# Retention and two MoE layers in one kernel: one tile per PSUM bank, w_out's combinations in layer 1, and more elementwise work on GpSimd

## The chip, the cores and the metric

One core of a Trainium2 chip runs the whole program. The metric is the device time of one execution in microseconds. The engines are named as in the profile: PE is TensorE, DVE is VectorE, ACT is ScalarE, POOL is GpSimd, SP is the engine whose queue issues almost all DMAs here.

## The reference

Three stages in a row, all in float32 (batch 4, 8 heads, 768 positions, head size 64, so 3072 tokens of 512 features; the hidden size of both layers is 2048):

```python
state = gamma * state + k_t (outer) v_t          # retention, per head, position by position
y_t   = scale * q_t @ state
h = y @ w_in;  P = a0 + a1*h + a2*h*h + a3*h**3;  Q = 1 + |b0|*|h| + |b1|*h*h     # layer 1
x = (P / (Q + 1e-6)) @ w_out
h = x @ w_in2;  g = h * clip(h + 3, 0, 6) / 6                                     # layer 2
out = g @ w_out2
```

The layer weights arrive as float64 and are rebuilt on the chip from their two 32-bit words.

## The kernel before, in words

**Split operands.** A factor is kept as a rounded high part (`hi`, made by ACT with a copy) and a rest (`lo` = value minus `hi`, made by one `tensor_tensor` subtract). A product is three matmuls: hi by hi, hi by lo, lo by hi.

**Layer 1.** Tokens are taken in six blocks of 512, the hidden size in 16 pieces of 128. A *step* is one piece of one block; there are 96 steps, written out by the main loop (line 1133 on), which in step n issues: 12 matmuls for h of step n (`emit_h`), ACT's three reads of the h before (`s1_h`), DVE's three operations for the gate of step n-2 (`s1_g`, lines 449 to 451), ACT's hi of that g (`s_hi`, line 456), then `s1_pq` (lines 434, 435, 438) with `s_lo` between its parts, which is the subtract that gives g's rest `gl` (line 462, on DVE), and 12 matmuls of step n-2 into the four output banks (`emit_o`, line 391). The last four of these 12 read `gl`; in the last step of a block they are interleaved, so that the third one reads it. The retention's chunks (`att_...`) and the rebuilding of layer 1's weights (`w_...`) are laid between the steps through the tables `begin`, `middle`, `between`, `before` and `after`: a call put there for step n is issued at that place of step n. Engines run what is issued to them strictly in order.

**Preparation of layer 2's weights.** Layer 2 uses a seven-product scheme on 2 by 2 halves of tokens, input and hidden pieces, so combinations of quarters of `w_in2` and `w_out2` are needed, each as hi and lo, and are stored to DRAM (`win_d`, `wout_d`). A half unit is: two loads (`prep_load`), one ACT operation (`prep_scale`), two on DVE (`prep_bits`, lines 559 and 560), four 128x128 sums on POOL (`prep_sums`), the hi copies on ACT (`prep_hi`) and the subtracts (`prep_lo`, line 601). For `w_in2` (16 half units) this is done in layer 1, five half units in the 16 steps from 32, 48 and 64 on and one at step 83, with the subtracts on DVE (two of 128x512). For `w_out2` (16 half units, in batches of 2 to 3) it is done in the first pair of layer 2, with the subtracts on POOL (one of 128x1024).

**Layer 2.** Blocks go in three pairs. `xc_load`, `xc_sums` and `xc_split` make the token combinations of a pair (for the first pair during steps 81 to 92, for the others late in the pair before). Then eight *units* (`unit`, hidden piece u of 8) make the gates: 7 groups of 6 matmuls (`mm1`, line 655) into PSUM banks A, B, C, D, with DVE sums of banks in between (line 531 through `tensor`) and a gate per quarter (`relu` on ACT, line 673; `gate` on DVE, line 679). A and D are the two halves of one tile, `live[p]` (profile name `ad`). Then come 14 *halves* of products, in the order `ORDER` = 1, 5, 6, 7, 3, 2, 4 with k = 0, 1; each is 48 matmuls of 128x256 (line 797). `g_split` makes the operand of a half two halves ahead: for each of four pieces j a source, then hi on ACT (line 771), then lo on DVE (line 531). For q = 5, 6, 7 and 3 the source is itself a sum or difference, made on DVE by `source` (line 758) just before. `evac` combines the banks into the output, and its place on DVE is between the splits:

```python
for i, (q, k) in enumerate(halves):
    product(p, q, k)
    if i: evac(p, *halves[i - 1])
    if i + 2 < len(halves): g_split(p, *halves[i + 2])
```

**PSUM** has eight banks: `accA` and `accB` (one tile of two banks each), `h` (two tiles of one), `at` (one tile of two). In layer 2 the product accumulators A and B lie in `accA` and `accB`, and C in `at`.

Of the kernel before, what the change touches and what calls it, by code (L numbers as in the profile page):

```python
# [16 lines left out]
CH = 128  # L17
# [15 lines left out]
def tile_retention_moe_moe2(  # L33
# [292 lines left out]

    def att_xh(blk, c):
        y = attn[blk, c][0].rearrange("p (e j t) -> p e j t", e=2, t=CH)[:, :, 0:2, :]
        xs = slice(c * CH, (c + 1) * CH)
        if blk == VIA:  # L330
            xf = o_p.tile([128, 512], F32, tag="osb", name=f"xf{blk}_{c}")
            nc.scalar.activation(split(by_pair(xf)), y, AF.Copy)
            nc.sync.dma_start(out=x_dram[:, :, xs].rearrange("a p t -> p a t"), in_=by_pair(xf))
        else:
            if c == 0:
                x_tiles(blk)
            nc.scalar.activation(split(xin[blk][0][:, :, xs]), y, AF.Copy)  # L337
# [35 lines left out]
    def emit_o(key):  # L373
# [241 lines left out]
    def xc_sums(p, c, which):  # L615
# [79 lines left out]
    def unit(p, u, part):  # L695
        nm = f"{p}_{u}"
        if part == 0:
            if u == 0:
                live[p] = ps_at.tile([128, 1024], F32, tag="at", name=f"ad{p}")
            now = live[p, u] = {"A": live[p][:, 0:512], "D": live[p][:, 512:1024]}  # L700
# [8 lines left out]
            tensor(nc.vector, now["U2"], now["B"], now["s1"], ALU.add)  # L709
            if u:  # L710
# [4 lines left out]
        else:  # L715
# [8 lines left out]
            gate(p, 22, u, h22, relu(h22, "22_" + nm))  # L724
            mm1(p, u, 4, now["D"], True)
# [18 lines left out]
    def source(p, q, k, j):  # L744
# [77 lines left out]
    def evac(p, q, k):  # L822
        ps = accs[p, BANK[q]][:, k * 512 : (k + 1) * 512]
# [7 lines left out]
        elif q == 7:  # L831
# [3 lines left out]
            scaled(o, accs[p, "C"][:, k * 512 : (k + 1) * 512], kept["U3", k])  # L835
# [37 lines left out]
    def wo_bits(v):  # L873
        for u, s in wo_batches[v] if v < len(wo_batches) else ():
# [3 lines left out]

    def wo_split(v):
        for u, s in wo_batches[v] if v < len(wo_batches) else ():  # L880
            hi = take(f"hwo{u}_{s}")
            prep_hi("wo", u, s, 2, hi)
            prep_lo("wo", u, s, nc.gpsimd)
            give(hi, *wo_rooms.pop((u, s)))

    def second_layer():
        for p in range(PAIRS):
            for u in range(NU):
                last = u == NU - 1
                if (p, u) != (0, 0):  # L890
                    unit(p, u, 0)
                    if not last:
                        win_load(p, u + 1)
                    if p == 0:
                        wo_load(u + 1)
                        wo_bits(u)
                    unit(p, u, 1)
                    if p == 0:
                        wo_split(u)
                if last:  # L900
                    wout_load(p, ORDER[0])
                    g_split(p, 1, 0, range(3))
            mm1(p, NU - 1, 3, live[p, NU - 1]["C"], False)
            last_two(p, NU - 1, 0)
            last_two(p, NU - 1, 1)
            g_split(p, 1, 0, (3,))
            give(*(t for q in ORDER for t in xs.pop((p, q))))
            jobs_x = xc_jobs(p + 1) if p + 1 < PAIRS else []
            g_split(p, *halves[1])
            for i, (q, k) in enumerate(halves):  # L910
# [8 lines left out]
                for fn, *args in jobs_x.pop(0) if i >= 7 and jobs_x else ():  # L919
# [5 lines left out]
    def xc_jobs(p):  # L925
        js = []
# [344 lines left out]
```

## Time and profile before

| what | us |
|---|---|
| median of 3 runs (lowest to highest) | 1313.13 (1311.78 to 1315.44) |
| the profiled execution's own time | 1309.85 |
| its span, first to last instruction | 1308.1 |
| PE busy | 1151.9 (88%) |
| DVE busy | 973.9 (74%) |
| ACT busy | 731.3 (56%) |
| POOL busy | 139.6 (11%) |
| mean granted clock of TensorE | 0.958 |

The profile is that of one execution; times in its rows count from the span's start. Layer 1's steps end near 657 us, the three pairs of layer 2 end near 901, 1105 and 1303 us. A row of a timeline gives start, duration, engine, line, operation, what it writes and reads, and in brackets the idle time of the engine before it and what ended that. A busy PE is not PE at its peak. The granted clock is the share of full speed.

### The profile page before, as it was taken

Reading aid. Unit: us, or ns where it says so; the run is one execution under the profiler, and the core shown is the slowest. Engines: PE = TensorE matmul, PEld = TensorE weight load, DVE = VectorE, ACT = ScalarE, POOL = GpSimd, SP = SyncE. Lnnn points to the kernel's source line nnn. Section 1 sums busy time; section 2 is a strip of 40 time slices with the busy share of each in tenths; the row PEclk is TensorE's granted clock in tenths of the full one; section 3 lists DMA queues with packets and bytes.
Section 4 is the critical chain, followed back from the end, with each engine's and each line's share of the span. In section 5 each row is a group of like instructions: output and inputs, shape, how many; then the busy total and the mean of one; then the engine's idle time right before and its main releaser. Section 6 shows DMA issues by size and latency. Waiting matters only on the chain.

```text
span 1308.1 us, 18580 instructions
## 1 busy us (share of the span) xinstructions
PE 1151.9 (88%) x6748; PEld 958.6 (73%) x6748; DVE 973.9 (74%) x1514; ACT 731.3 (56%) x1309; POOL 139.6 (11%) x179
## 2 busy tenths in 40 slices
PE   8789999999999999998985679778888779888878
PEld 5567888887788777786764568677677779667778
DVE  6898999989989889999874456675556675556663
ACT  3999888677777777777653334342224343233341
POOL 0221110011101101200037550000000000000000
PEclk9899999999999999999997789989999989999989
DMA  9898444134344434434439996348733437832433
GB/s 340 244 249 219 103 114 145 47 132 131 128 136 154 129 106 147 136 105 145 129 104 339 335 316 211 127 135 303 285 113 106 152 113 234 330 128 98 162 112 113
DMA packets 133099, 224.13 MB, mean 171 GB/s; under 512 B 9744, under 2 KB 75408, under 8 KB 133008
## 3 DMA queue, kind: packets, MB, share of 16 engines
q1 hardware_dynamic: 128832, 215.35, 49.2%
q0 software_dynamic: 4176, 7.60, 3.5%
q8 instruction: 53, 0.87, 0.3%
q14 instruction: 38, 0.31, 0.1%
HBM read 167.08 MB, written 48.23 MB: 165 GB/s over the span
## 4 chain that ended last, share of the span: by engine, by line
PE 38%; DVE 31%; ACT 16%; issue 7%; DMA 6%; SPq 1%; POOL 0%; ACTq 0%; DVEq 0%; POOLq 0%
PE h L370 8%; PE ad L655 5%; PE hB L655 5%; ACT s L771 5%; DVE s L531 4%; PE accA L391 4%; PE hC L655 4%; PE accB L391 4%; DVE S L531 3%; PE mA L797 3%; DVE p L450 2%; DVE u L435 2%; DVE u L449 2%; PE mC L797 2%; DVE p L434 2%
## 5 line engine op out<-in xcount | busy, mean ns | idle before, releaser
L370 PE MATMUL h<-xh,wi 128*128 128x512 f32 x768 | 211.4, 397 | 0.9 <-ACT xh L337 0.9
L370 PEld LDWEIGHTS h<-xh,wi 128*128 128x128 f32 x768 | 141.5, 188 | 34.2 <-issue 2.8
L797 PE MATMUL mB<-wo,s 128*128 128x256 f32 x864 | 118.8, 298 | 25.5 <-issue 15.5
L391 PE MATMUL accA<-gh,wo 128*128 128x512 f32 x384 | 122.4, 400 | 16.7 <-ACT gh L456 16.0
L797 PEld LDWEIGHTS mB<-wo,s 128*128 128x128 f32 x864 | 113.0, 204 | 30.8 <-issue 20.4
L391 PE MATMUL accB<-gh,wo 128*128 128x512 f32 x384 | 119.4, 392 | 0.0
L655 PE MATMUL ad<-x,wih 128*128 128x512 f32 x160 | 52.4, 448 | 59.2 <-DVE U L531 39.5
L771 ACT ACTIVATE s<-S 128x512 fp32r<-128x512 f32 x72 | 45.5, 631 | 103.9 <-DVE S L531 103.9
L370 PE MATMUL h<-xl,wi 128*128 128x512 f32 x384 | 103.3, 391 | 0.0
L797 PE MATMUL mC<-wo,s 128*128 128x256 f32 x576 | 82.7, 310 | 21.5 <-DVE o L820 10.6
L391 PEld LDWEIGHTS accA<-gh,wo 128*128 128x128 f32 x384 | 70.5, 189 | 40.8 <-ACT gh L456 27.4
L797 PEld LDWEIGHTS mC<-wo,s 128*128 128x128 f32 x576 | 80.5, 219 | 23.4 <-ACT s L771 12.2
L443 ACT ACTIVATE r<-u,cst 128x512 f32<-128x512 f32 x96 | 69.3, 722 | 46.9 <-DVE u L435 46.9
L531 DVE TENSOR_TENSOR s<-S,s 128x512 fp32r<-128x512 f32 x72 | 49.9, 693 | 52.1 <-ACT s L771 52.1
L456 ACT ACTIVATE gh<-p 128x512 fp32r<-128x512 f32 x96 | 60.6, 632 | 47.2 <-DVE p L451 47.2
L655 PEld LDWEIGHTS ad<-x,wih 128*128 128x128 f32 x160 | 31.3, 208 | 75.2 <-DVE U L531 47.6
L673 ACT ACTIVATE r<-U,cst 128x512 f32<-128x512 f32 x48 | 34.6, 721 | 92.1 <-DVE U L531 92.1
L391 PEld LDWEIGHTS accB<-gh,wo 128*128 128x128 f32 x384 | 72.7, 189 | 15.7
L370 PEld LDWEIGHTS h<-xl,wi 128*128 128x128 f32 x384 | 72.4, 189 | 15.9
L434 DVE TENSOR_TENSOR p<-p,h 128x512 f32<-128x512 f32 x96 | 65.6, 683 | 23.6 <-ACT u L428 23.4
L797 PE MATMUL mA<-wo,s 128*128 128x256 f32 x576 | 75.5, 292 | 6.7 <-ACT s L771 3.1
L797 PEld LDWEIGHTS mA<-wo,s 128*128 128x128 f32 x576 | 73.1, 199 | 9.1 <-ACT s L771 4.2
(163 smaller groups left out, 2438.8 us busy)
## 6 DMA issues: line engine op xcount, KB each, us to landing
wo<-wout SPq DMA_DIRECT2D x84, 512.0 KB, 6.0
wih<-win SPq DMA_DIRECT2D x48, 512.0 KB, 6.8
wil<-win SPq DMA_DIRECT2D x48, 512.0 KB, 7.1
T<-in_qk_t_dram SPq DMA_DIRECT2D x48, 256.0 KB, 4.6
rwi<-in_moe_w_in_dram SPq DMA_DIRECT2D x16, 512.0 KB, 5.2
rwo<-in_moe_w_out_dram SPq DMA_DIRECT2D x16, 512.0 KB, 5.1
kv<-in_kv_dram SPq DMA_DIRECT2D x32, 256.0 KB, 5.4
pwi<-in_moe_w_in_dram SPq DMA_DIRECT2D x32, 256.0 KB, 4.3
```

The lines of the kernel that those rows point to most:

```text
L370: nc.tensor.matmul(ps, lhsT=w[:, cs], rhs=x[:, c, :], start=n == 0, stop=n == 3 * KD - 1)
L391: nc.tensor.matmul(acc[layer, blk][j], lhsT=l, rhs=r, start=f == f0 and i == 0, stop=f == f1 and i == 2)
L434: nc.vector.tensor_tensor(out=p, in0=p, in1=h, op=ALU.mult)
L435: nc.vector.scalar_tensor_tensor(out=u, in0=s, scalar=babs[:, 1:2], in1=u, op0=ALU.mult, op1=ALU.add)
L443: nc.scalar.activation(r, u, AF.Ln, scale=1.0 / LN_SCALE, bias=ln_bias)
L449: nc.vector.scalar_tensor_tensor(out=u, in0=u, scalar=Q_CONST, in1=r, op0=ALU.add, op1=ALU.mult)
L456: nc.scalar.activation(gh, tm[key], AF.Copy)
L531: engine.tensor_tensor(out=out, in0=a, in1=b, op=op)
L655: nc.tensor.matmul(bank, lhsT=wl[p, u][c][a][:, slot], rhs=xs[p, q][b][:, c * 512 : (c + 1) * 512], start=start and i == 0 and c == 0, sto ...
L673: nc.scalar.activation(r, h, AF.Relu, bias=three)
L771: nc.scalar.activation(hi, src, AF.Copy)
L797: nc.tensor.matmul(out, lhsT=l, rhs=r, start=q in (1, 4, 5, 6) and t == 0 and f == 0 and i == 0, stop=f == NU - 1 and i == 2, skip_group_c ...
```

## The change

Six edits:

1. **Banks.** The four output banks of layer 1 become four tiles `acc0` to `acc3`; in layer 2 the accumulators A and B lie in these by half k, and C in the two `h` tiles. D of a unit gets the tile `acc0`, apart from A, except in the very first unit. Retention's first block uses `acc0` to `acc3` too, so that its copies and masks over two banks become two instructions each.
2. **g's rest** (`s_lo`) goes from DVE to POOL, in all 96 steps.
3. **Preparation.** `prep_lo` of `w_in2` goes from DVE to POOL and writes new tiles of the pool `osb` (3 buffers) and not in place. The half units go faster (nine per 16 steps), and 15 of the 16 half units of `w_out2` follow in layer 1: 10 among the same steps up to 78 and five at steps 82 to 90. One is left for the first pair.
4. **Token combinations** (`xc_sums`) go from DVE to POOL; their loads come earlier, and their splits are spread three to a half.
5. **Half of g's sums** (`source`, j = 1 and 3) go from DVE to POOL.
6. **Order.** A unit is issued in three parts where it was two, cut after U2; the last piece of the first split comes before the last unit's closing operations.

The core of the diff:

```diff
     def two_banks(blk, i, name):
...
+        if blk == 0 and i < 2:
+            banks = [ps_acc.tile([128, 512], F32, tag=f"acc{2 * i + e}", name=f"{name}_{e}") for e in range(2)]
+            return banks, banks
...
     def emit_o(key):
...
-                t[:, i * 512 : (i + 1) * 512]
-                for t in (ps_acc.tile([128, 1024], F32, tag=f"acc{s}", name=f"acc{s}{layer}_{blk}_{f}") for s in "AB")
-                for i in range(2)
+                ps_acc.tile([128, 512], F32, tag=f"acc{j}", name=f"acc{layer}_{blk}_{f}_{j}") for j in range(KD)
...
     def s_lo(key):
-        nc.vector.tensor_tensor(out=gl, in0=tm.pop(key), in1=gh.bitcast(F32), op=ALU.subtract)
+        nc.gpsimd.tensor_tensor(out=gl, in0=tm.pop(key), in1=gh.bitcast(F32), op=ALU.subtract)
...
-    def prep_lo(kind, u, s, engine):
+    def prep_lo(kind, u, s, engine, in_place=False):
...
+        for part, (at, hi) in enumerate(done):
+            cs = slice(at, at + 512)
+            if in_place:
+                lo = raw[:, cs]
+            else:
+                lo = o_p.tile([128, 512], F32, tag="osb", name=f"lo{kind}{u}_{s}_{part}")
+            tensor(engine, lo, raw[:, cs], f32(hi), ALU.subtract)
+            prep_store(kind, u, s, cs, 1, lo)
...
     def unit(p, u, part):
...
-                live[p] = ps_at.tile([128, 1024], F32, tag="at", name=f"ad{p}")
-            now = live[p, u] = {"A": live[p][:, 0:512], "D": live[p][:, 512:1024]}
+                live[p] = ps_at.tile([128, 1024], F32, tag="at", name=f"a{p}")
+            now = live[p, u] = {"A": live[p][:, 0:512]}
...
+            if (p, u) == (0, 0):
+                now["D"] = live[p][:, 512:1024]
+            else:
+                now["D"] = ps_acc.tile([128, 512], F32, tag="acc0", name="hD" + nm)
             mm1(p, u, 4, now["D"], True)
...
     def source(p, q, k, j):
-            tensor(nc.vector, to, a, b, op)
+            tensor(nc.gpsimd if j % 2 else nc.vector, to, a, b, op)
...
     def product(p, q, k):
-        if k == 0 and q in (1, 6, 5):
-            pool, tag = {"A": (ps_acc, "accA"), "B": (ps_acc, "accB"), "C": (ps_at, "at")}[b]
-            accs[p, b] = pool.tile([128, 1024], F32, tag=tag, name=f"m{b}{p}")
+        if q in (1, 6, 5):
+            pool, tag = {"A": (ps_acc, f"acc{k}"), "B": (ps_acc, f"acc{2 + k}"), "C": (ps_h, "h")}[b]
+            accs[p, b, k] = pool.tile([128, 512], F32, tag=tag, name=f"m{b}{p}_{k}")
...
     def second_layer():
...
                     unit(p, u, 0)
+                    unit(p, u, 1)
                     if not last:
                         win_load(p, u + 1)
                     if p == 0:
-                        wo_load(u + 1)
-                        wo_bits(u)
-                    unit(p, u, 1)
+                        wo_load(u)
+                        wo_bits(u - 1)
+                    unit(p, u, 2)
                     if p == 0:
-                        wo_split(u)
+                        wo_split(u - 1)
...
+        js = {5: [(xc_load, p, 0)], 6: [(xc_load, p, 1)]}
...
+            js[7 + c] = [(xc_sums, p, c, 0, nc.gpsimd), (xc_sums, p, c, 1, nc.gpsimd)]
...
-    starts = [b + i for b in (32, 48, 64) for i in (3, 5, 8, 10, 12)] + [83]
...
+    halves_due = [(kind, u, i) for kind in ("wi", "wo") for u in range(NU) for i in range(2)]
+    starts = [b + i for b in (32, 48, 64) for i in (2, 3, 5, 6, 8, 9, 11, 12, 14)][1:]
+    for n, job in zip(starts, halves_due):
+        put(begin, n, prep_load, *job)
+        put(middle, n + 1, prep_scale, *job)
+        put(between, n + 1, prep_bits, *job)
+        put(before, n + 1, prep_sums, *job)
+        put(before, n + 1, prep_hi, *job, 0)
+        put(middle, n + 2, prep_hi, *job, 1)
+        put(before, n + 2, prep_lo, *job, nc.gpsimd)
+    wo_units = halves_due[len(starts) :]
+    wo_batches = {n: [wo_units.pop(0)[1:]] for n in (-14, -12, -10, -8, -6, 1)}
+    for n in (-14, -12, -10, -8, -6):
...
+    for c, n in enumerate((84, 89)):
+        put(begin, n, xc_load, 0, c)
+        put(before, n + 1, xc_sums, 0, c, 0, nc.gpsimd)
+        put(before, n + 2, xc_sums, 0, c, 1, nc.gpsimd)
```

## Rows read from the trace of the kernel before

**Rows 1.** Busy time by stretch: length; PE, PEld, DVE, ACT, POOL; granted clock; DMA share.

```profile
core 0: us, PE busy (x) PEld busy (x) DVE busy (x) ACT busy (x) POOL busy (x), PEclk, DMA share, GB/s
...
244.10:559.00 314.90, 306.63 (x1858) 245.19 (x1857) 286.55 (x443) 232.87 (x441) 37.06 (x60) 1.00 0.39 129
569.90:657.20 87.30, 79.86 (x337) 62.05 (x337) 79.16 (x124) 61.97 (x105) 2.45 (x4) 1.00 0.37 121
...
674.40:791.00 116.60, 83.33 (x301) 64.38 (x301) 62.06 (x92) 48.48 (x71) 69.71 (x72) 0.82 1.03 319
791.00:901.00 110.00, 91.65 (x673) 88.35 (x673) 76.24 (x121) 42.20 (x74) 0.00 (x0) 0.92 0.49 169
901.00:994.00 93.00, 80.19 (x336) 63.50 (x336) 46.69 (x71) 26.59 (x41) 0.00 (x0) 0.98 0.54 198
994.00:1105.40 111.40, 92.92 (x674) 89.90 (x672) 76.72 (x122) 42.67 (x75) 0.00 (x0) 0.91 0.46 159
...
1196.10:1303.20 107.10, 90.48 (x673) 87.33 (x671) 63.23 (x100) 35.07 (x61) 0.00 (x0) 0.92 0.40 133
```

**Rows 2.** Timeline of PE in layer 1: the first matmuls of two neighbouring steps.

```profile
216.87 1.07 PE L370 MATMUL h<-xh,wi 128*128 128x512 f32 x4
...
222.31 1.07 PE L370 MATMUL h<-xh,wi 128*128 128x512 f32 x4
```

**Rows 3.** Waits of the whole span: us in total, times, longest.

```profile
ACT s L771 <- DVE S L531: 103.9, 71, 2.9
...
PE ad L655 <- DVE U L531: 39.5, 19, 5.7
```

**Rows 4.** Timeline of PE, second pair: first and last unit that waits.

```profile
914.68 1.20 PE L655 MATMUL ad<-x,wih 128*128 128x512 f32 x4 [1.51 <-DVE U L531]
...
982.98 1.19 PE L655 MATMUL ad<-x,wih 128*128 128x512 f32 x4 [1.57 <-DVE U L531]
```

**Rows 5.** Timeline of PE, first pair: the start of two of its units.

```profile
710.46 0.77 PE L655 MATMUL ad<-x,wih 128*128 128x512 f32 x1 [6.92 <-DMA wih<-win]
...
778.07 2.07 PE L655 MATMUL ad<-x,wih 128*128 128x512 f32 x4 [3.53 <-DVE U L531]
```

**Rows 6.** Timeline of DVE, second pair, split of a half with q = 7.

```profile
1036.77 0.69 DVE L531 TENSOR_TENSOR s<-g,s 128x512 fp32r<-128x512 f32 x1 [0.78 <-ACT s L771]
1037.38 0.69 DVE L531 TENSOR_TENSOR g<-g,g 128x512 f32<-128x512 f32 x1
1038.77 0.69 DVE L531 TENSOR_TENSOR s<-g,s 128x512 fp32r<-128x512 f32 x1 [0.70 <-ACT s L771]
```

**Rows 7.** Timeline of PE, second pair: halves (7, 0), (7, 1), (3, 0), (3, 1).

```profile
1044.22 7.46 PE L797 MATMUL mB<-wo,s 128*128 128x256 f32 x48 [5.16 <-issue]
1052.99 5.99 PE L797 MATMUL mB<-wo,s 128*128 128x256 f32 x48 [1.31 <-DVE e L820]
1062.23 8.53 PE L797 MATMUL mC<-wo,s 128*128 128x256 f32 x48 [3.25 <-issue]
1074.89 7.47 PE L797 MATMUL mC<-wo,s 128*128 128x256 f32 x48 [4.12 <-DVE o L820]
```

**Rows 8.** Groups by line: busy us, mean ns of one, idle before.

```profile
L462 DVE TENSOR_TENSOR gl<-p,gh 128x512 fp32r<-128x512 f32 x96 | 65.8, 685 | 11.9 <-ACT gh L456 11.8
L434 DVE TENSOR_TENSOR p<-p,h 128x512 f32<-128x512 f32 x96 | 65.6, 683 | 23.6 <-ACT u L428 23.4
```

**Rows 9.** The same view: POOL's subtracts and sums.

```profile
L531 POOL TENSOR_TENSOR pwo<-pwo,hwo 128x1024 f32<-128x1024 f32 x16 | 39.8, 2513 | 0.0
L531 POOL TENSOR_TENSOR pwi<-pwi 128x128 f32<-128x128 f32 x64 | 39.5, 638 | 362.4 <-DVE pwi L560 329.7 <-ACT r L443 31.4
```

**Rows 10.** Timelines of POOL and DVE, near 293 and 781 us.

```profile
292.46 3.07 POOL L531 TENSOR_TENSOR pwi<-pwi 128x128 f32<-128x128 f32 x4 [12.77 <-DVE pwi L560]
292.85 0.74 DVE L438 SCALAR_TENSOR_TENSOR p<-p,ab,h 128x512 f32<-128x512 f32 x1
294.27 0.95 DVE L449 SCALAR_TENSOR_TENSOR u<-u,r 128x512 f32<-128x512 f32 x1
...
777.69 4.72 POOL L531 TENSOR_TENSOR pwo<-pwo,hwo 128x1024 f32<-128x1024 f32 x2
781.08 1.89 DVE L679 SCALAR_TENSOR_TENSOR g<-r,U 128x512 f32<-128x512 f32 x1 [3.06 <-DMA wout<-hwo]
```

More of the change, by code (lines that the diff above doesn't have):

```diff
@@ L325, in split, with outputs @@
         return t.rearrange("p (e j) t -> p e j t", e=2)
+    def outputs(blk, c, to):
+        banks = attn[blk, c][0]
+        if len(banks) == 1:
+            y = banks[0].rearrange("p (e j t) -> p e j t", e=2, t=CH)
+            return [(y[:, :, 0:2, :], split(to))]
+        return [(by_pair(b)[:, 0:2, :], to[:, 2 * e : 2 * e + 2, :]) for e, b in enumerate(banks)]
     def att_xh(blk, c):
-        y = attn[blk, c][0].rearrange("p (e j t) -> p e j t", e=2, t=CH)[:, :, 0:2, :]
         xs = slice(c * CH, (c + 1) * CH)
@@ L336, in att_xh @@
                 x_tiles(blk)
-            nc.scalar.activation(split(xin[blk][0][:, :, xs]), y, AF.Copy)
+            to = xin[blk][0][:, :, xs]
+        for y, x in outputs(blk, c, to):
+            nc.scalar.activation(x, y, AF.Copy)
+        if blk == VIA:
+            nc.sync.dma_start(out=x_dram[:, :, xs].rearrange("a p t -> p a t"), in_=by_pair(xf))
     def att_xl(blk, c):
-        both = attn[blk, c][0]
         if blk != VIA:
-            y = both.rearrange("p (e j t) -> p e j t", e=2, t=CH)[:, :, 0:2, :]
-            xh, xl = (split(x[:, :, c * CH : (c + 1) * CH]) for x in xin[blk])
-            nc.vector.tensor_tensor(out=xl, in0=y, in1=xh.bitcast(F32), op=ALU.subtract)
+            xh, xl = (x[:, :, c * CH : (c + 1) * CH] for x in xin[blk])
+            for (y, h), (_, lo) in zip(outputs(blk, c, xh), outputs(blk, c, xl)):
+                nc.vector.tensor_tensor(out=lo, in0=y, in1=h.bitcast(F32), op=ALU.subtract)
     def att_state(blk, c):
@@ L613, in xc_load, with xc_sums @@
         xraw[p, c] = [a, b]
-    def xc_sums(p, c, which):
+    def xc_sums(p, c, which, engine):
         a, b = xraw[p, c][:2]
@@ L709, in unit @@
             tensor(nc.vector, now["U2"], now["B"], now["s1"], ALU.add)
+        elif part == 1:
+            now = live[p, u]
             if u:
@@ L873, in wo_bits @@
     def wo_bits(v):
-        for u, s in wo_batches[v] if v < len(wo_batches) else ():
+        for u, s in wo_batches.get(v, ()):
             prep_scale("wo", u, s)
@@ L877, in wo_bits, with wo_done @@
             prep_sums("wo", u, s)
+    def wo_done(v):
+        give(*wo_rooms.pop(wo_batches[v][0]))
     def wo_split(v):
-        for u, s in wo_batches[v] if v < len(wo_batches) else ():
+        for u, s in wo_batches.get(v, ()):
             hi = take(f"hwo{u}_{s}")
             prep_hi("wo", u, s, 2, hi)
-            prep_lo("wo", u, s, nc.gpsimd)
+            prep_lo("wo", u, s, nc.gpsimd, True)
             give(hi, *wo_rooms.pop((u, s)))
@@ L918, in second_layer @@
                     g_split(p, *halves[i + 2])
-                for fn, *args in jobs_x.pop(0) if i >= 7 and jobs_x else ():
+                for fn, *args in jobs_x.get(i, ()):
                     fn(*args)
@@ L1043, in tile_retention_moe_moe2 @@
     put(before, 94, win_load, 0, 1)
-    put(before, 95, wo_load, 0)
-    put(before, N1, wo_load, 1)
-    put(before, N1 + 1, wo_bits, 0)
-    put(after, N1 + 1, wo_split, 0)
     nc.scalar.preload_act_table_set("natural_log_exp_and_others")
@@ L1187, in tile_retention_moe_moe2 @@
         if not cur:
-            unit(0, 0, n - N1)
+            unit(0, 0, 2 * (n - N1))
         o = at_step(n - LAG)
@@ L1193, in tile_retention_moe_moe2 @@
                 late.append(o)
+        if n == N1:
+            unit(0, 0, 1)
         for fn, *args in after.get(n, ()):
```

70 lines of the change are left out of this document (29 added, 41 removed).

## Prediction, made before the changed kernel was run

> **What bounds the kernel now.** I read the busy time by stretch first. In layer 1 (the stretches 244 to 559 and 570 to 657 of [rows 1]) PE is busy 306.6 of 314.9 us and 79.9 of 87.3: layer 1 is nearly PE's, with 8.3 and 7.4 us to gain. A step without retention takes 5.44 us for 24 matmuls [rows 2], 0.227 us each. DVE is at 91% there, so it is close behind. Layer 2 is another matter. A pair's eight units hold 336 matmuls (76.2 us at 0.227) and its 14 halves 83.9 us at the 5.99 us of an undisturbed half (the one at 1052.99 in [rows 7]); the rows show 93.0 and 111.4 us for the second pair, and 116.6 us for seven units of the first with a granted clock of 0.82 [rows 1].
>
> Then the waits tell what stands in PE's way. In the units PE waits for DVE's U, 39.5 us in all [rows 3]. The unit's first matmuls go to bank A, yet the wait ends when DVE has read bank D of the unit before: a wait between two halves of one tile. It comes once in each of seven units of the second pair, from the first to the last of [rows 4], 1.5 to 1.6 us each, and the same in the third pair. In the first pair waits are longer and partly for a weight load [rows 5]: there the DMAs run at full share, 1.03 [rows 1], because w_out2 is loaded and stored beside them.
>
> In the products DVE sets the pace. In a half with q = 5, 6, 7 or 3 each piece goes source (DVE), hi (ACT), lo (DVE), in order, and DVE idles 0.70 to 0.78 us while ACT makes hi [rows 6]; one piece takes 2.0 us (1036.77 to 1038.77), a half 8.0 us against PE's 5.99. ACT waits as long for the sources, 103.9 us in all [rows 3]. PE's stalls of 5.16 and 3.25 us follow, and after a stall a half takes 7.46 to 8.53 us, not 5.99 [rows 7].
>
> **The change part by part**, against the profiled execution's 1309.85 us.
>
> *D apart from A.* The wait for D's reader goes. Next to come on A would be the reader of bank A's last gate, three groups of matmuls (18 x 0.227 = 4.1 us) earlier by the code's order, and DVE's and ACT's work in a unit (nine and five operations of about 0.7 us) fits in 9.5 us. So a unit goes to 42 x 0.227 = 9.5 us from 11.38 (982.98 less 914.68, over 6). I count the seven idle times of 1.57 alone: **-11 in the second and in the third pair, -22**. Bounds: -18 (part comes back as a wait for hi copies) to -26 (7 x 1.86 x 2).
>
> *First pair's units.* All but one half unit of w_out2 leaves. Seven units at 9.5 are 67 us; the loads for the third unit are issued behind layer 1's last stores, which I price at 6 us, just under the worst load wait of 6.92 [rows 5]. So 73 where 116.6 stood: **-44**. Bounds -47 (no such wait) and -36 (two of them). With the DMAs gone the U waits of 3.5 us stay covered by D's tile; in the very first unit D still shares A's tile and that wait stays.
>
> *Half of g's sums on POOL.* Now two pieces of four keep 2.0 us and two cost DVE only their lo, 0.61 us apart [rows 6]: a half is 5.2 us, eight halves 42 where 64 stood, -22 for a pair. POOL's sources are not free. No row shows POOL on 128x512. Half of a 128x1024 piece is 1.26 us, four 128x128 ones are 2.55 [rows 9]; I take 1.26, since 1024 elements cost four times, not eight times, as much as 128, so long pieces are the cheaper. Two per half lie beside DVE's idle 0.7 us and delay the next lo by about 0.5 us each (next paragraph): +8 for eight halves. Late halves cost less after that: halves (3, 0) and (3, 1) took 4.0 us over 5.99 each and waited 4.1 more [rows 7]; I give that 4 us. **-18 a pair, -54** in all. Bounds: the products can't go below 83.9 from 110.0, 111.4 and 107.1 [rows 1], so -77; if POOL's 2.55 holds, about -30.
>
> *What DVE and POOL cost each other.* VectorE's 0.69 us gate with both inputs in SBUF took 1.89 us beside a pair of POOL subtracts and ended 0.56 us after them (782.97 and 782.41); beside the 128x128 sums an operation with two SBUF inputs took 0.95 us, while one that reads PSUM kept 0.74 [rows 10]. The Trainium skill (SBUF — State Buffer, "Who interferes with whom") says that a VectorE instruction with two SBUF inputs and a GpSimd instruction that reads SBUF exclude each other for a whole instruction, whichever is first, and that VectorE with one SBUF input is free of it. The rows agree, and by that rule the work of both adds up below, where by the 0.25 us of the 0.95 row alone layer 1 would have room and fall by some 16 us.
>
> *Layer 1.* DVE loses g's rest (0.685 us a step [rows 8]) and the w_in2 subtracts, and gains 10 more half units' bit operations. In 244 to 559 lie 48 steps and, now, 26 half units. POOL: 48 x 1.26 + 26 x (2 x 1.26 + 4 x 0.64 [rows 9]) = 193 us. DVE with two SBUF inputs: four of a step's six (the two others, as line 434 [rows 8], read PSUM) and one per half unit, 218 x 0.61 = 133. Together 326 us in a stretch of 314.9: +11 if nothing overlaps, and some 4 for what waits behind: g's rest stands in POOL's queue behind subtracts that wait for ACT's hi; ACT's second hi waits for POOL's sums and for one of three `osb` buffers (a half unit now fills four), with the next step's logarithm queued behind; SP's next load stands behind the store of a rest. **+15**, bounds -8 (PE's idle time goes) and +40 (durations of 0.69 to 0.75 in place of 0.61, and twice the queueing). In 570 to 657: POOL 15 + 8 pieces of 1.26 and 5 half units of 5.1, 54 us; DVE 60 + 14 + 5 operations, 48; 102 in 87.3. The half units end at step 92, so I take two thirds of the excess: **+10**, bounds -7 and +25. Before 244 us g's rest fits between DVE's PSUM reads and its wait for ACT: 0, bounds -5 and +5; the doubled copies of retention's first block are in this.
>
> *At no cost:* xc_sums on POOL in the later pairs (behind the splits of q = 2 and 4, where DVE has only four lo's a half); the unit in three parts and the earlier first split (issue order alone, hidden by PE's 9.5 us). If that cover went, each costs one wait of 1 to 2 us a pair.
>
> Sum: -22 - 44 - 54 + 15 + 10 = -95, so 1215 for that execution; the median of the runs stood 3.3 above it: **1218 us**.
>
> **The rivals.**
>
> *Sharing, not exclusion.* DVE's work is only stretched as in the 0.95 row, layer 1 gains its 16 us and the products run at PE's pace (-75): 1218 - 41 - 21 = **1156**. For it: most DVE operations beside POOL stretch little. Against: the 1.89. Chance 0.11.
>
> *The exclusion bites harder.* POOL at 1.9 us a piece, midway between its bounds: layer 1 +60, products -10 a pair: 1218 + 35 + 24 = **1277**. For it: g's rest has to be there 1.8 us after hi (eight matmuls). Chance 0.16.
>
> *D's reader still holds A, or the next wait is as long.* The units of the later pairs stay at 11.4, the U waits of the first pair at part: 1218 + 25 = **1243**. Chance 0.07.
>
> *Slower.* In steps 32 to 96 POOL's queue never empties, so that each g's rest comes late, PE waits for it in every step and DVE's next gate with it: POOL's 4.0 us a step (193 over 48) and DVE's six operations plus retention (4.7) then follow one another, 8.7 us a step where 6.56 stand (314.9 over 48). 64 steps lose 2.1 each, 137 us: 1218 - 25 + 137 = **1330**. It decides from 1.9 us a step on, where layer 2's 120 us are eaten up. For it: POOL and DVE together are over the stretch's length. Against: DVE reads PSUM or waits for ACT for a third of a step, and the lag of two steps between h and its output leaves slack. Chance 0.05.
>
> **How the numbers follow.** The forecast has 0.61. The range takes its bounds (layer 1 by -45 to +45, the products by -23 to +24, seldom together) and reaches halfway into the first two rivals: 1166 to 1276. A difference under 0.3%, 4 us, can't be told from none: only the last rival is slower, 0.05; 0.01 for none; faster 0.94.
>
> **What would show it.** Right: PE's idle before bank A's first matmuls under 0.3 us in the later pairs, unit starts 9.5 to 9.8 us apart; the first pair's seven units near 73 us with the granted clock above 0.9; products near 92 us a pair; `gl` on POOL at 1.2 to 1.4 us; layer 1's two stretches longer, with PE waiting for `gl` or `gh`. Wrong: layer 1 no longer than before, or PE waiting in each step for POOL; splits still 8 us a half.

## The result, and the profile after

The changed kernel takes 1255.96 us (median of four runs, 1251.32 to 1259.28) where the kernel before takes 1312.45 beside it: a ratio of 0.9563, interval 0.9528 to 0.9598, so 4.4% faster. The forecast was 1218, range 1166 to 1276. The profiled execution took 1256.97 us, its span is 1255.2, 52.9 less than before.

Busy time by stretch of the changed kernel, with the columns of [rows 1]. The stretches are the same pieces of work: steps 2 to 31, 32 to 79, the end of layer 1, units two to eight of the first pair, its products, then units and products of the second pair and of the third.

```profile
core 0: us, PE busy (x) PEld busy (x) DVE busy (x) ACT busy (x) POOL busy (x), PEclk, DMA share, GB/s
45.00:251.40 206.40, 193.56 (x1105) 153.15 (x1106) 181.72 (x258) 176.36 (x332) 64.40 (x56) 0.98 0.60 158
251.40:601.40 350.00, 315.39 (x1857) 247.07 (x1855) 321.99 (x387) 249.96 (x473) 217.05 (x200) 0.99 0.53 165
615.20:716.10 100.90, 82.19 (x333) 61.90 (x331) 88.11 (x105) 67.06 (x113) 63.48 (x52) 0.98 0.48 151
733.40:809.50 76.10, 70.86 (x299) 57.02 (x297) 43.04 (x66) 26.55 (x43) 6.05 (x7) 0.96 0.67 231
809.50:906.80 97.30, 88.54 (x673) 86.88 (x674) 75.88 (x98) 39.93 (x73) 37.97 (x23) 0.93 0.56 186
906.80:984.20 77.40, 76.81 (x337) 62.62 (x336) 45.93 (x71) 26.36 (x41) 0.00 (x0) 1.00 0.59 221
984.20:1081.00 96.80, 87.03 (x673) 84.57 (x674) 76.34 (x98) 40.49 (x74) 39.77 (x24) 0.96 0.58 193
1081.00:1158.20 77.20, 76.84 (x338) 62.64 (x336) 46.01 (x71) 26.22 (x41) 0.00 (x0) 1.00 0.60 222
1158.20:1251.00 92.80, 85.51 (x672) 82.87 (x672) 62.33 (x84) 33.00 (x60) 27.05 (x16) 0.98 0.48 157
```

Layer 2 gives back time in every stretch; the stretch of 314.9 in layer 1 has become 350.0, that of 87.3 100.9. DVE has an eighth fewer instructions in the long stretch (387, before 443), yet is busy longer: 322.0 us, before 286.6 [rows 1]. Two views say why. (The lines have moved a little: the gate's three operations on DVE, 449 to 451 before, are now 454 to 456, lines 435 and 438 are 440 and 443, and g's rest is line 467.) The groups by line, changed kernel (busy us, mean ns of one, idle before):

```profile
L467 POOL TENSOR_TENSOR gl<-p,gh 128x512 fp32r<-128x512 f32 x96 | 143.6, 1496 | 254.3 <-ACT gh L461 170.9
L440 DVE SCALAR_TENSOR_TENSOR u<-s,babs,u 128x512 f32<-128x512 f32 x96 | 98.3, 1024 | 0.0
L454 DVE SCALAR_TENSOR_TENSOR u<-u,r 128x512 f32<-128x512 f32 x96 | 85.9, 895 | 33.7 <-ACT r L449 33.7
L455 DVE SCALAR_TENSOR_TENSOR p<-p,ab,r 128x512 f32<-128x512 f32 x96 | 91.6, 955 | 0.0
```

and its timelines of DVE and of POOL near 310 us (start, duration):

```profile
309.05 1.45 DVE L454 SCALAR_TENSOR_TENSOR u<-u,r 128x512 f32<-128x512 f32 x1 [0.86 <-ACT r L449]
310.42 1.76 DVE L455 SCALAR_TENSOR_TENSOR p<-p,ab,r 128x512 f32<-128x512 f32 x1
312.21 0.69 DVE L456 SCALAR_TENSOR_TENSOR p<-u,p 128x512 f32<-128x512 f32 x1
...
314.08 1.52 DVE L564 TENSOR_SCALAR pwi<-pwi 128x512 int32<-128x512 int32 x1
...
316.32 0.74 DVE L443 SCALAR_TENSOR_TENSOR p<-p,ab,h 128x512 f32<-128x512 f32 x1
```

```profile
308.65 2.98 POOL L536 TENSOR_TENSOR lowi<-pwi,hiwi 128x512 f32<-128x512 f32 x2
313.65 1.67 POOL L467 TENSOR_TENSOR gl<-p,gh 128x512 fp32r<-128x512 f32 x1 [2.02 <-ACT gh L461]
316.48 1.83 POOL L536 TENSOR_TENSOR pwi<-pwi 128x128 f32<-128x128 f32 x4 [1.17 <-DVE pwi L565]
```

Read the two side by side. While POOL runs its two subtracts (308.65 to 311.63), DVE's lines 454 and 455, whose two inputs lie in SBUF, take 1.45 and 1.76 us; line 456, after POOL has stopped, takes 0.69. Line 443 reads PSUM and keeps its 0.74 beside POOL's sums. By means over the whole kernel, lines 454, 455 and 440 stand at 895, 955 and 1024 ns, where they have 724, 781 and 753 in a run below (e8) that has g's rest and the subtracts on DVE.

In layer 2 the false wait, that of bank A for the reader of the other half of its tile, is gone: the view of waits has no wait of PE for U any more (39.5 us in [rows 3]), and two neighbouring units of the second pair start 9.52 us apart (timeline of PE):

```profile
919.84 1.07 PE L666 MATMUL a<-x,wih 128*128 128x512 f32 x4
...
929.36 1.07 PE L666 MATMUL a<-x,wih 128*128 128x512 f32 x4
```

In the products DVE still sets the pace. Timelines of DVE and of POOL, changed kernel, second pair, to be held against [rows 6]:

```profile
1010.49 1.78 DVE L536 TENSOR_TENSOR S<-S,g 128x512 f32<-128x512 f32 x1
1013.04 2.62 DVE L536 TENSOR_TENSOR s<-S,s 128x512 fp32r<-128x512 f32 x2 [0.78 <-ACT s L788]
1015.59 1.77 DVE L536 TENSOR_TENSOR S<-S,g 128x512 f32<-128x512 f32 x1
1018.14 1.53 DVE L536 TENSOR_TENSOR s<-S,s 128x512 fp32r<-128x512 f32 x2 [0.78 <-ACT s L788]
1019.59 0.68 DVE L536 TENSOR_TENSOR S<-S,g 128x512 f32<-128x512 f32 x1
```

```profile
1008.27 6.84 POOL L536 TENSOR_TENSOR g<-g,g 128x512 f32<-128x512 f32 x4
1015.08 3.44 POOL L536 TENSOR_TENSOR S<-g,S 128x512 f32<-128x512 f32 x2
1019.75 1.67 POOL L536 TENSOR_TENSOR S<-g,S 128x512 f32<-128x512 f32 x1 [1.23 <-DVE s L536]
```

DVE's source takes 1.77 us where POOL is already running and 0.68 at 1019.59, where POOL stands still from 1018.52 to 1019.75; POOL's pieces take 1.7. The 0.78 us in which DVE waits for ACT's hi is still there, once per two pieces.

### The profile page after: what moved, and what is told of

Same layout as the page of the kernel before. It is cut to its first block, busy times and chain, and to the rows that moved or that the text cites. A ratio compares the mean times of both kernels' runs of the same rounds, so it can differ in the third digit from the quotient of the medians.

```text
span 1255.2 us, 18982 instructions
## 1 busy us (share of the span) xinstructions
PE 1137.7 (91%) x6748; PEld 943.1 (75%) x6748; DVE 995.5 (79%) x1319; ACT 729.2 (58%) x1327; POOL 470.6 (37%) x395
## 4 chain that ended last, share of the span: by engine, by line
DVE 37%; PE 33%; ACT 13%; issue 9%; DMA 4%; POOL 2%; SPq 0%; ACTq 0%; DVEq 0%; POOLq 0%
DVE s L536 7%; PE a L666 5%; PE acc L396 5%; PE hB L666 4%; PE hC L666 4%; DVE u L440 4%; DVE p L455 4%; DVE u L454 4%; PE h L377 4%; DVE p L439 3%; PE mB L814 3%; PE mA L814 3%; DVE S L536 3%; ACT s L788 2%; ACT r L448 2%
## 5 line engine op out<-in xcount | busy, mean ns | idle before, releaser
L396 PE MATMUL acc<-gh,wo 128*128 128x512 f32 x768 | 203.2, 403 | 40.2 <-ACT gh L461 39.9
L467 POOL TENSOR_TENSOR gl<-p,gh 128x512 fp32r<-128x512 f32 x96 | 143.6, 1496 | 254.3 <-ACT gh L461 170.9
L396 PEld LDWEIGHTS acc<-gh,wo 128*128 128x128 f32 x768 | 143.2, 191 | 86.0 <-ACT gh L461 57.6
L536 POOL TENSOR_TENSOR S<-g,g 128x512 f32<-128x512 f32 x12 | 20.0, 1695 | 277.5 <-DVE s L536 227.9
L814 PE MATMUL mB<-wo,s 128*128 128x256 f32 x864 | 111.8, 290 | 13.5 <-issue 7.2
L396 PE MATMUL acc<-gl,wo 128*128 128x512 f32 x384 | 110.2, 401 | 8.2 <-POOL gl L467 8.2
L454 DVE SCALAR_TENSOR_TENSOR u<-u,r 128x512 f32<-128x512 f32 x96 | 85.9, 895 | 33.7 <-ACT r L449 33.7
L440 DVE SCALAR_TENSOR_TENSOR u<-s,babs,u 128x512 f32<-128x512 f32 x96 | 98.3, 1024 | 0.0
L396 PEld LDWEIGHTS acc<-gl,wo 128*128 128x128 f32 x384 | 74.0, 193 | 27.4 <-POOL gl L467 11.2
L455 DVE SCALAR_TENSOR_TENSOR p<-p,ab,r 128x512 f32<-128x512 f32 x96 | 91.6, 955 | 0.0
L814 PEld LDWEIGHTS mC<-wo,s 128*128 128x128 f32 x576 | 77.1, 209 | 14.6 <-ACT s L788 9.6
L536 DVE TENSOR_TENSOR s<-S,s 128x512 fp32r<-128x512 f32 x72 | 64.0, 928 | 27.0 <-ACT s L788 27.0
```

The costliest lines, as they stand in the source:

```text
L396: nc.tensor.matmul(acc[layer, blk][j], lhsT=l, rhs=r, start=f == f0 and i == 0, stop=f == f1 and i == 2)
L440: nc.vector.scalar_tensor_tensor(out=u, in0=s, scalar=babs[:, 1:2], in1=u, op0=ALU.mult, op1=ALU.add)
L454: nc.vector.scalar_tensor_tensor(out=u, in0=u, scalar=Q_CONST, in1=r, op0=ALU.add, op1=ALU.mult)
L455: nc.vector.scalar_tensor_tensor(out=p, in0=p, scalar=ab[:, 0:1], in1=r, op0=ALU.add, op1=ALU.mult)
L467: nc.gpsimd.tensor_tensor(out=gl, in0=tm.pop(key), in1=gh.bitcast(F32), op=ALU.subtract)
L536: engine.tensor_tensor(out=out, in0=a, in1=b, op=op)
```

## The experiments

All were run beside the kernel before (medians 1313.1 to 1314.0), so the ratios compare. The table has the lengths of the stretches in each run's trace: steps of layer 1 from the first matmul for h of one step to that of another, the end of layer 1, the eight units and the products of each pair (us).

| kernel | median | ratio (interval) | steps 2-31 | 32-79 | 80-end | units 1 | products 1 | units 2 | products 2 | units 3 | products 3 |
|---|---|---|---|---|---|---|---|---|---|---|---|
| before | 1313 | 1 | 199.1 | 314.9 | 97.7 | 134.3 | 110.0 | 93.0 | 111.4 | 90.7 | 107.1 |
| changed | 1256.0 | 0.9563 (.9528-.9598) | 206.5 | 350.0 | 114.6 | 93.4 | 97.3 | 77.4 | 96.8 | 77.2 | 92.8 |
| e2_banks_alone | 1281.7 | 0.9756 (.9739-.9774) | 198.9 | 315.4 | 97.7 | 134.5 | 109.8 | 78.3 | 109.6 | 77.3 | 105.1 |
| e1_rest_on_dve | 1234.9 | 0.9397 (.9380-.9413) | 199.0 | 340.5 | 107.9 | 93.8 | 96.6 | 77.3 | 96.8 | 77.5 | 92.8 |
| e3_sources_dve | 1289.8 | 0.9816 (.9798-.9834) | 205.8 | 351.2 | 114.6 | 92.4 | 108.9 | 77.1 | 107.4 | 77.3 | 106.6 |
| e4_wout_late | 1263.4 | 0.9612 (.9594-.9630) | 205.9 | 333.0 | 96.4 | 137.5 | 95.7 | 77.2 | 96.8 | 77.3 | 92.8 |
| e6_lo_on_dve | 1231.5 | 0.9378 (.9354-.9403) | 200.4 | 338.8 | 106.7 | 91.8 | 96.6 | 77.1 | 96.8 | 77.4 | 92.8 |
| e7_lo_in_place | 1230.6 | 0.9366 (.9338-.9393) | 199.2 | 335.5 | 107.7 | 93.3 | 94.8 | 77.2 | 97.2 | 77.6 | 92.8 |
| e8_lo_dve_in_place | 1226.3 | 0.9337 (.9303-.9370) | 198.8 | 332.3 | 106.7 | 92.9 | 94.2 | 77.7 | 98.5 | 77.4 | 92.8 |
| e9_xc_on_dve | 1233.9 | 0.9395 (.9367-.9422) | 202.0 | 340.6 | 107.1 | 91.9 | 94.8 | 77.2 | 98.5 | 77.4 | 92.8 |
| e10_wout_partly_late | 1224.0 | 0.9308 (.9279-.9338) | 199.9 | 336.4 | 101.0 | 99.8 | 95.7 | 77.9 | 96.7 | 77.2 | 92.8 |
| e11_sources_ahead_dve | 1188.6 | 0.9048 (.9020-.9076) | 201.2 | 330.8 | 106.2 | 93.2 | 85.0 | 77.3 | 83.5 | 77.4 | 81.2 |
| e12_both | 1191.1 | 0.9064 (.9035-.9094) | 202.1 | 333.8 | 101.2 | 99.0 | 83.5 | 77.2 | 83.5 | 78.7 | 81.2 |
| e13_sources_ahead_half | 1210.3 | 0.9215 (.9190-.9240) | 199.5 | 331.8 | 107.0 | 92.5 | 90.5 | 77.6 | 91.8 | 77.6 | 90.1 |

**One part at a time.** My theory was that POOL's work in layer 1 holds DVE up and that the other parts pay. The rival was that the moved half units themselves are the cost.

*g's rest back on DVE*, all else as changed:

```diff
-        nc.gpsimd.tensor_tensor(out=gl, in0=tm.pop(key), in1=gh.bitcast(F32), op=ALU.subtract)
+        nc.vector.tensor_tensor(out=gl, in0=tm.pop(key), in1=gh.bitcast(F32), op=ALU.subtract)
```

> The changed kernel with g's rest (s_lo) back on DVE in all 96 steps, nothing else. Theory A (DVE and POOL exclude each other, so layer 1 pays for each POOL piece): 96 pieces of 1.3 us leave POOL and DVE gets 0.61 us a step, so layer 1 ends some 25 us earlier, near 690 us where the changed kernel has 716, and the whole is near 1230. Theory B (layer 1 is longer because of the work moved into it, on DVE, ACT and SP): DVE gets 59 us more to do, layer 1 stays at 716 or ends later, 1256 to 1275. Theory C (g's rest is late in POOL's queue): only the 8 us that PE waits for gl come back, about 1248.

Measured 1234.9, 21 us under the changed kernel: layer 1 is 23.7 us shorter, and steps 2 to 31 are back at 199.0, all of their 7.5. So edit 2, in this kernel, costs 24 us of layer 1, and a third of that comes before step 32, where POOL has no half units in its queue.

*The banks alone*: the kernel before with edit 1 only (`acc0` to `acc3`, D in `acc0`, C in the `h` tiles).

```diff
-            now = live[p, u] = {"A": live[p][:, 0:512], "D": live[p][:, 512:1024]}
+            now = live[p, u] = {"A": live[p][:, 0:512]}
...
+                now["D"] = ps_acc.tile([128, 512], F32, tag="acc0", name="hD" + nm)
```

> The kernel before with the PSUM edit alone: four tiles acc0 to acc3, D of a unit in acc0, C in the two h tiles. If the wait for D's reader is what stood before bank A: unit starts of the second and third pair 9.5 us apart, 13 to 16 us less for each, some 10 us in the first pair, products and layer 1 within 2 us of before, in all near 1275. If another wait takes its place: within 5 us of before.

Measured 1281.7. The units of the second and third pair lose 14.7 and 13.4 us, those of the first nothing (134.5), where I had expected some 10. The first pair's stretch and the start of one of its units (timeline of PE) in this run:

```profile
673.00:807.00 134.00, 98.23 (x399) 77.91 (x400) 75.63 (x113) 56.77 (x84) 70.92 (x74) 0.83 0.96 304
```

```profile
710.52 0.77 PE L660 MATMUL ad<-x,wih 128*128 128x512 f32 x1 [6.75 <-DMA wih<-win]
712.96 1.65 PE L660 MATMUL ad<-x,wih 128*128 128x512 f32 x3 [1.68 <-DMA wih<-win]
```

With the DMAs at 0.96 of their time PE waits for weights instead of for bank D: from 657 to 791 us its waits for DVE's U fall from 17.7 us before to 1.4, and those for the weights of `wih` rise from 16.8 to 32.4. So the wait of 3.53 us in [rows 5] stood in front of a wait for the transfers, and the split of the banks gives nothing there until w_out2 has left.

*All sources on DVE*: `tensor(nc.vector, to, a, b, op)` in `source`, all else as changed.

> The changed kernel with all of g's sums (source) back on DVE. If the move of half of them is what shortened the products: 12 to 15 us longer for each of three pairs, near 1296. If the bank tiles or the later placed token combinations did it: within 10 us of the changed kernel.

Measured 1289.8, products 108.9, 107.4 and 106.6. So edit 5 is worth 11.6, 10.6 and 13.8 us, 36 in all; the other 5.6 that the products gained are not its doing, and no run shows what gave them.

*w_out2 back in the first pair*: its 16 half units in the batches of before, the places of w_in2 in layer 1 as changed.

```diff
-    halves_due = [(kind, u, i) for kind in ("wi", "wo") for u in range(NU) for i in range(2)]
+    halves_due = [("wi", u, i) for u in range(NU) for i in range(2)]
...
+    wo_units = [(u, s) for u in range(NU) for s in range(2)]
+    wo_batches = dict(enumerate([wo_units.pop(0) for _ in range(n)] for n in (2, 3, 3, 2, 2, 2, 2)))
```

> The changed kernel with all 16 half units of w_out2 back in the first pair of layer 2, in the batches of before; the 16 of w_in2 keep their places, so layer 1 has half units in steps 35 to 60 and none after. Theory A and theory B alike: layer 1's later steps lose most of their excess, about 22 us of 29 from step 65 on; what is left, about 0.3 us a step, belongs to g's rest and the token combinations on POOL by A, and nothing is left by B. The first pair's units get about 30 us longer. In all near 1264.

Measured 1263.4. The first pair's units go to 137.5 and layer 1 ends at 680.0, 36.1 us sooner than in the changed kernel (716.1). Moving w_out2's combinations buys 44 us and costs 36: nearly a wash while g's rest and the subtracts are on POOL. The rival is part of the truth.

**What is left in layer 1.** These four stand on e1 (g's rest on DVE). *The subtracts of both weights on DVE too*, still into the three `osb` tiles:

```diff
-        put(before, n + 2, prep_lo, *job, nc.gpsimd)
+        put(before, n + 2, prep_lo, *job, nc.vector)
```

> e1 (g's rest on DVE) with the preparation's subtracts in layer 1 on DVE as well, still into osb tiles. Theory A (exclusion): POOL loses 62 pieces of 1.3 us, DVE gets 62 of 0.61; if each POOL piece costs DVE about its own length, layer 1 ends 15 to 25 us earlier, near 672, the whole near 1215. Theory B (work moved in, DVE full): DVE's 38 us more show, layer 1 ends some 10 us later, the whole near 1245.

*The subtracts on POOL, but in place* (`prep_lo, *job, nc.gpsimd, True`), so that no `osb` tile has to come free:

> e1 with the preparation's rests written in place, so that a half unit fills two osb tiles and not four, and the raw tile is held until its store has landed. If the three osb tiles are what holds ACT (its 5 us waits for a landing store of a rest and what follows, steps 44, 60 and 76 at 10 to 12 us): these steps come to 9 us and the whole to about 1226. If they only move, to ACT's wait for the next load into raw: 1230 to 1240.

*Both: on DVE and in place* (`prep_lo, *job, nc.vector, True`):

> e1 with the preparation's subtracts on DVE and in place: e6 and e7 together. By A with the osb limit: the sum of both gains, near 1210. If raw is what binds instead: as e6 or slower.

*The token combinations of the first pair on DVE* (`xc_sums, 0, c, 0, nc.vector`):

> e1 with the first pair's token sums (xc_sums) back on DVE: eight pieces of 1.3 us leave POOL in steps 85 to 91, DVE gets eight of 0.61. By A: steps 80 to the end 4 to 6 us shorter than e1's 108 us. If those steps are bound by the amount of DVE's work: 3 to 5 us longer.

Layer 1 ends at 692.4 in e1, 690.6 in e6, 687.0 in e7, 682.7 in e8 and 694.7 in e9. I summed DVE's durations above the undisturbed ones of the same operation in steps 32 to 79: 77 us in the changed kernel, 45 in e1, 9 in e6, 10 in e8, 5 before. So taking the subtracts off POOL removes 36 us of waiting on DVE (e6 against e1), but DVE then makes them itself, 52 of 0.69 us, and layer 1 gains 2 us where one theory had 15 to 25 and the other a loss of 10: on which of the two engines they run matters little. The three tiles seem to cost something too. Timelines of ACT and POOL in e1:

```profile
438.17 0.63 ACT L591 ACTIVATE hiwi<-pwi 128x512 fp32r<-128x512 f32 x1 [3.28 <-DMA win<-lowi]
438.71 0.71 ACT L448 ACTIVATE r<-u,cst 128x512 f32<-128x512 f32 x1
```

```profile
438.63 2.66 POOL L536 TENSOR_TENSOR lowi<-pwi,hiwi 128x512 f32<-128x512 f32 x2 [6.35 <-DMA win<-lowi]
```

ACT's second hi waits 3.28 us for the store of a rest to land, and the gate's logarithm (line 448) is queued behind it. In place ACT has no such wait in e7's trace, and layer 1 ends 5.4 us sooner there, 9.7 with the subtracts on DVE as well (e8). By the medians e6 and e7 (1231.5 and 1230.6) can't be told apart, and their intervals overlap with that of e1 (1234.9); only both together (e8, 1226.3) are clear of it. So how the 9.7 us divide between the engine and the tiles is not shown, and a pool of four tiles was not tried. The place of the token combinations makes no difference that these runs can tell (e9, 1233.9 against 1234.9): the end of layer 1 is 107.1 us for 107.9, neither the 4 to 6 less of the one theory nor the 3 to 5 more of the other.

The 26 us that e8 still has over the kernel before I put down to the moved work, by counting; no run takes it out of e8 as a whole. In steps 32 to 79 it now has 26 half units where 15 were; each takes DVE 0.42 + 3 x 0.69 = 2.5 us, so 11 more are 27 us, and DVE is busy 313.1 us in e8 where it was 286.6:

```profile
243.70:576.00 332.30, 312.70 (x1858) 244.94 (x1857) 313.13 (x485) 249.85 (x474) 67.11 (x103) 0.99 0.54 174
```

That is 94% of the stretch. PE is busy as long, 312.7 us, but its matmuls are those of before, and its waits for the `gh` that follows DVE's gate are twice as long (32.3 us for 16.0; the lines stand under the rivals below). So DVE is, as far as these numbers go, what holds layer 1 up now.

**A better split between layer 1 and the first pair?** On e8, the last three of the five half units that follow step 80 go back to the first pair, which then has four: `wo_batches` for `(-14, -12, 1, 2, 3, 4)`.

> e8 with three more half units of w_out2 (from steps 86, 88 and 90) and the one before them left to the first pair, so four there, one in each of the units 1 to 4, where e8 has one. Theory B (the work moved into layer 1 is what is left of its excess, about 2 us a half unit near the end): steps 80 to the end fall from 106.7 to about 101, and the first pair, whose DVE and ACT are half idle, grows by less than 4 us: about 1223. If DMA in the first pair is full again with one half unit a unit: it grows by 8 us or more, about 1230.

Measured 1224.0 against 1226.3: the end of layer 1 gains 5.7, as expected, and the first pair's units lose 6.9, between the two figures expected (under 4, and 8 or more). In all there is no difference that these runs can tell.

**The products: too much work for DVE, or a bad order?** The 0.78 us beside ACT suggested the order. On e8, the four sources of a half are issued ahead of its four hi and lo, and all four are made on DVE (the engine's line is changed as in e3):

```diff
-        for j in js:
-            src = source(p, q, k, j)
+        srcs = [source(p, q, k, j) for j in js]
+        for j, src in zip(js, srcs):
```

> e8 with g's sums all on DVE again, but a half's four sources issued before its first lo, so that DVE need not wait for ACT between them. If the products of before were slow because of the chain source, hi, lo on two engines in order: a half costs DVE eight operations of 0.61 us, 4.9 us and an evac, under PE's 5.8, and the products come to 85 to 89 us a pair, in all near 1203. If DVE's amount of work was the limit, as e3 alone would also allow: 107 us a pair as in e3, in all near 1260.

The same with j = 1 and 3 of the sources on POOL, as in the changed kernel:

> e8 with the sources issued ahead as in e11, half of them still on POOL. By exclusion POOL's two pieces of 1.3 us now meet DVE operations in a row with no idle time beside them: DVE needs six operations of 0.61 and up to two of 1.3 us, 6.3 us a half with evac 6.9: products 90 to 95 us a pair, slower than e11 by some 15 us in all. If only the order matters: as e11 within 3 us.

And e10 and e11 together:

> e10 and e11 together: the sum of their differences to e8, 1198 to 1205 where both hold.

Measured 1188.6 (e11), 1210.3 (e13), 1191.1 (e12). The products of e11 fall to 85.0, 83.5 and 81.2 us, below the 85 to 89 expected, and e11 and e12 take less than the 1203 and the 1198 to 1205 that were expected of them. Timelines of DVE and of PE in e11, second pair:

```profile
969.80 0.67 DVE L837 SCALAR_TENSOR_TENSOR e<-mB,e 128x512 f32<-128x512 f32 x1
970.40 2.48 DVE L536 TENSOR_TENSOR g<-g,g 128x512 f32<-128x512 f32 x4
972.81 2.59 DVE L536 TENSOR_TENSOR s<-g,s 128x512 fp32r<-128x512 f32 x4
975.31 0.68 DVE L837 SCALAR_TENSOR_TENSOR e<-mB,e 128x512 f32<-128x512 f32 x1
```

```profile
961.79 23.20 PE L814 MATMUL mB<-wo,s 128*128 128x256 f32 x192
984.83 5.92 PE L814 MATMUL mC<-wo,s 128*128 128x256 f32 x48
```

A whole half, nine operations, now takes DVE 5.51 us (969.80 to 975.31) without a gap, under PE's 5.99; PE runs 192 matmuls, four halves, on end in 23.20, 5.80 each; 14 of these are 81.2 us, so nothing is left to gain from DVE here. The eight operations of a split alone took 8 us in the old order [rows 6]: it was the wait for ACT, four times a half, and not DVE's load. With that gone, POOL's help does harm: e13 has the same order and its products are 90.1 to 91.8, since DVE's operations spend 24.6, 25.4 and 18.1 us of the three pairs' products above their undisturbed durations (e11: 8.4, 8.1 and 0.7). E11 is 5.4% below the changed kernel by the two medians (1188.6 and 1256.0), and the fastest that I ran; e12 is not to be told from it.

## Why the prediction was right, and where it was not

The sign, the range and the shape held: layer 2 gains, layer 1 loses, less than that. The time was 38 us too low: of a forecast gain of 95 us 56.5 came. (The forecast of 44 us for the first pair is for its units two to eight; the table has all eight.) By the terms, forecast and then measured on the profiled executions:

| term | forecast | measured |
|---|---|---|
| D apart from A, second and third pair | -22 | -29.1 (15.6 and 13.5) |
| first pair's units | -44 | -40.9 |
| products, three pairs | -54 | -41.6 (12.7, 14.6, 14.3) |
| layer 1 before step 32 | 0 | +7.4 |
| steps 32 to 79 (stretch of 314.9) | +15 | +35.1 |
| the end of layer 1 (step 80 on) | +10 | +16.9 |
| sum | -95 | -52.2 |

*D apart from A*: right in mechanism (e2 alone gives -28.1), under-sized, and beyond the bound of -26. I counted the idle time of 1.57 us and not the slower matmuls behind it: the unit went from 11.38 to 9.52 us, which is the 1.86 that I had kept for the bound. The other 3 us lie at the start of a pair, where PE waited for its first weights in the kernel before (timeline of PE) and does not in the changed one:

```profile
903.01 0.96 PE L655 MATMUL ad<-x,wih 128*128 128x512 f32 x3 [1.78 <-DMA wih<-win]
```

*First pair*: right, seven units in 76.1 us for the forecast 73, at a granted clock of 0.96 where 0.82 stood. It is w_out2's leaving that does it: e4 has the banks apart and w_out2 there, and takes 137.5. The bounds of this term don't follow from its own prices: 116.6 less 67 is 50 without the wait of 6 us and 38 with two of them, not 47 and 36.

*Products*: the mechanism was right (e3), the price of POOL's meeting too low. I took 0.5 us a meeting; the rows show a DVE source at 1.77 us where 0.68 is undisturbed, 1.1 us each. The price of POOL alone was right: 1.26 forecast, 1.28 to 1.30 measured where DVE is out of its way; the 1.50 that `gl` takes on average holds its waiting for DVE. One that ran beside no operation of DVE (timeline of POOL, changed kernel):

```profile
118.09 1.29 POOL L467 TENSOR_TENSOR gl<-p,gh 128x512 fp32r<-128x512 f32 x1 [8.47 <-issue]
```

What I had not seen is that the whole gain was to be had by order alone, from the 0.70 to 0.78 us that I quoted from [rows 6].

*Layer 1 is the step that failed.* First, "g's rest fits between DVE's PSUM reads and its wait for ACT: 0" before step 32: measured +7.4, and e1 returns it. POOL is busy there for less than a third of the time, and still DVE's operations spend some 20 us above their undisturbed durations (2 in e1): free time on both engines doesn't keep them apart. Second, the sum "326 us in a stretch of 314.9", which added POOL's work to the DVE operations that share its port. I took it for the length; the length is DVE's own: 245 us of its own operations (322.0 busy less the 77 above undisturbed), 77 of standing behind POOL and 28 of idle time, 350 in all. DVE works in order, so its reads of PSUM and its waits for ACT don't move to where POOL is busy. Only part of POOL's 217 us lay beside them. Held against e8, where DVE makes all of it, POOL's help took 58 us of work off DVE in this stretch (245 where e8 has 303) and made it stand 67 us longer (77 for 10). For the end of layer 1 the same sum, 102 us, was near the 100.9 measured, which is chance where the sum is not the length; by that stretch of 87.3 the term came to +13.6 for the +10 forecast, and the table's +16.9 is from step 80 on.

By cause, of layer 1's +59.4 us, in the order in which the runs undo them: g's rest on POOL 23.7 (e1), then the subtracts on POOL and their three tiles 9.7 (e8), and what e8 still has, 26.0, which I put down to the moved half units. In another order the shares differ: w_out2's half units taken out first are 36.1 (e4). The moved work I had counted only through the port, not as work of DVE and ACT in a stretch where DVE was at 91%.

*The rivals.* Exclusion against sharing: layer 1 did not gain 16 us but lost 59, VectorE's operations with two inputs in SBUF took up to 1.8 us for 0.7, and the two of a step that read PSUM were not slowed at all (lines 439 and 443 keep means of 0.68 and 0.74 us), so "sharing" is out. The rival in which the exclusion bites harder (1277) was the direction of the miss, and its +60 for layer 1 is even what came, but by luck: its reason, POOL at 1.9 us a piece, was wrong, for POOL is at 1.28 alone and 1.5 to 1.7 by waiting for DVE. The Trainium skill (SBUF — State Buffer, "Who interferes with whom") says that the one which starts second stands until the first is through, and this trace agrees in the main: 1.45 and 1.76 us beside POOL (lines 454 and 455) and 0.69 for line 456 without it; the last section has what is left over. "D's reader still holds A" is out by the 9.52 us. The slower rival needed PE to wait in every step for g's rest; the waits show 8.2 us in all for POOL's `gl`:

```profile
PE acc L396 <- ACT gh L461: 39.9, 31, 3.7
...
PE acc L396 <- POOL gl L467: 8.2, 7, 1.7
```

The 39.9 us for `gh` are DVE's gates being late. The same wait in the kernel before, and then in e8 (views of waits):

```profile
PE accA L391 <- ACT gh L456: 16.0, 17, 3.5
```

```profile
PE acc L396 <- ACT gh L461: 32.3, 25, 3.5
```

## What to carry to other kernels

Give two things that are read at different times a PSUM tile each, even where both fit one: here the shared tile cost 1.86 us a unit. Before work goes to GpSimd because VectorE sets the pace, see whether VectorE is busy or waits in order for another engine; where it waits, issue the independent first operations ahead of the dependent ones. And price a GpSimd operation that reads SBUF at what it takes from VectorE as well, up to 1.1 us for a piece of 128x512 here, unless VectorE reads PSUM or stands idle at that moment.

## What the runs showed of the hardware

An operation of VectorE with a single input is held up too, if it is the integer `tensor_scalar` of line 564: 1.52 us at 314.08, and by groups, first in the changed kernel and then in e8:

```profile
L564 DVE TENSOR_SCALAR pwi<-pwi 128x512 int32<-128x512 int32 x16 | 18.9, 1178 | 0.0
```

```profile
L564 DVE TENSOR_SCALAR pwi<-pwi 128x512 int32<-128x512 int32 x16 | 6.7, 421 | 0.2 <-DMA pwi<-in_moe_w_in_dram 0.2
```

The Trainium skill (SBUF — State Buffer, "Who interferes with whom") frees an operation with one SBUF input only outside the modes that use both ports, and names `tensor_scalar` among those that can contend. The prediction had left this condition out and counted only operations with two inputs.

And the exclusion is not quite the sum of both. In e13, where xc_sums and four lo run against one another, DVE takes 6.64 us for four and POOL 1.58 to 1.74 for each, so the pair of them takes some 1.7 us where 0.69 + 1.28 are 1.97 (1.89 with the 0.61 us that lie between two starts of undisturbed ones in [rows 6]):

```profile
998.62 6.64 DVE L536 TENSOR_TENSOR s<-S,s 128x512 fp32r<-128x512 f32 x4 [0.18 <-ACT s L788]
```

```profile
998.01 1.58 POOL L536 TENSOR_TENSOR xc<-xa 128x512 f32<-128x512 f32 x1 [13.93 <-PE mB L814]
999.67 1.63 POOL L536 TENSOR_TENSOR xc<-xb,xc 128x512 f32<-128x512 f32 x1
1001.26 1.74 POOL L536 TENSOR_TENSOR xd<-xb,xa 128x512 f32<-128x512 f32 x1
```

So 0.2 to 0.3 us of each pair lie beside one another, and the one that waits stands for somewhat less than the whole of the other's instruction.
